# A fused block-sparse attention and gated-MLP kernel: other load sizes, one copy on another engine, and another deal of products over ten slots

## The chip, the cores and the metric

The kernel runs on one core of a Trainium2 chip. The core has a matrix engine (TensorE, PE in the profile, with its weight loads as PEld), a vector engine (VectorE, DVE), a scalar engine (ScalarE, ACT), a general engine (GpSimd, POOL), and SyncE (SP), which here only issues transfers. Each engine works through its own queue in order. Transfers run on 16 DMA engines that the queues share. The metric is the time of one execution in microseconds of device time; lower is better. The median before is 209.31 us, from three runs between 209.13 and 209.51.

## The reference

Attention with a block mask runs over 4 batches, 8 heads, 768 tokens and 64 features a head; its output, with the heads side by side (512 features), goes through a gated MLP whose gate mixes over the tokens.

```python
scores = scale * np.matmul(q, k.transpose(0, 1, 3, 2))
mask = ...                       # neighbours, first and last block, 3 sampled blocks per row of blocks
attn = softmax(np.where(mask, scores, -1000000000.0))
x = matmul(attn, v) -> [4, 768, 512]

h = np.maximum(x @ w_in, 0.0)    # 512 -> 1024
u, v = h[..., :512], h[..., 512:]
v_n = (v - mean(v)) / sqrt(var(v) + 1e-06)
v_s = np.einsum('ts,bsd->btd', w_spatial, v_n) + b_spatial[None, :, None]
out = (u * v_s) @ w_out          # 512 -> 512
```

## The kernel before, in words

Work is laid out by hand in slots. `qk_unit` (slots 0 to 35) and `qk_full` (slots 36 to 179) put one piece of scores on TensorE in each slot, into one of two PSUM buffers of the tag `sc`, and one exponential of it on ScalarE (L479, L491). `av_full` multiplies the exponentials of seven slots before with v (L538). So in a slot from 43 on, TensorE has two score matmuls (L487), six with v, and after these as many gMLP matmuls as `run_queue` takes from a queue. For slots 20 to 97 the table `STEPS` (L817) says how many; after that they are dealt evenly. At slots 82 to 91 the queue holds the output products of batch 0.

The gMLP of a batch is a list of products. For each of six rows of 128 tokens there is v0 to v5 and u0 to u5 (four matmuls with `w_in_t` each), then six matmuls with the spatial weights `w_spt` (`s_product`), then four with `w_out_t` (`o_product`). A product ends with a copy out of PSUM: relu for u and v, bias and gate for s, and for o a copy to `osb` that is then stored. `O_ACT` (L625) names, for each of the first three batches, the rows whose copy out ScalarE makes; the others go to VectorE. `ST_ACT` names the rows whose store is issued from ScalarE's queue in place of SyncE's (row 4 of batch 2). Each row of v gets mean and variance on VectorE, then 1/sqrt(var) on GpSimd (`std`, `rstd`, L657 and L659), then the normalisation on VectorE (`vn<-vn,mv,rstd`, L188).

`last_x` runs after the attention slots. It drains what is left of batch 2 and opens batch 3: three of four matmuls of v0 and v1, then the output products of rows 4 and 5 of batch 2, then three of u0, and then the fourth of each. From there gMLP products take their PSUM buffers in turn from three pools (`tail_tags`), `sc` among them; rows 3, 4 and 5 of batch 2 have `sc` buffers too, and so has u0.

The weights come in through staging tiles. The spatial weights are 768 x 768 numbers, in six pieces of 384 KB: `ws_load` (L576) fetches one or two pieces, `ws_cast` casts one to bf16 on GpSimd in slots 19 to 29, and `ws_tr` transposes a pair by DMA. `w_out` has four pieces of 256 KB: `w_out_load` in slot 44, casts on GpSimd in slot 52. SyncE issues all of these in the order of the program, between the loads of q, k and v (L110), the transposes and the stores.

Of the kernel before, what the change touches and what calls it, by code (L numbers as in the profile page):

```python
# [10 lines left out]
FP32 = mybir.dt.float32  # L11
# [15 lines left out]
def kernel(  # L27
# [16 lines left out]
    nc = tc.nc  # L44

    B, H, S, D = q.shape
# [5 lines left out]
    DM = H * D  # L52
# [3 lines left out]
    NDH = DH // 128  # L56
# [14 lines left out]
    work = ctx.enter_context(tc.tile_pool(name="work", bufs=1))  # L71
# [155 lines left out]
    wst = {}  # L227

    def w_load(key, src):
        wst[key] = work.tile([128, DM], FP32, tag="osb", bufs=6, name="w_f")  # L230
        nc.sync.dma_start(out=wst[key], in_=src)
# [13 lines left out]

    def w_out_load(g):
        w_load(("o", g), moe_w_out[g * 128:(g + 1) * 128, :])

    def w_out_cast(g, eng):
        eng.tensor_copy(out=w_out_t[:, g, :], in_=wst.pop(("o", g)))  # L250
# [323 lines left out]
    ws = {}  # L574

    def ws_load(i, n=1):  # L576
        t = work.tile([128, n, S], FP32, tag=f"ws_f{n}", bufs=2, name="ws_f")
        nc.sync.dma_start(out=t, in_=moe_w_spatial.rearrange("(p c) s -> p c s", c=NCH)[:, i:i + n])
        for k in range(n):
            ws["f", i + k] = t[:, k]  # L580
# [41 lines left out]
        return out  # L622

    NORM_AT = {1: 23, 0: 23, 3: 36, 2: 36}
    O_ACT = [(4,), (0, 2, 4), (0, 2, 4)]  # L625
    ST_ACT = [(), (), (4,), (0, 1, 2)]
    VN_AGE, VN_STEP = 9, 2
    post = []
# [1 line left out]
    class Moe:  # L630
# [75 lines left out]
        def o_product(self, tcc):  # L706
# [4 lines left out]
            for i in range(parts):  # L711
                cs = slice(i * w, (i + 1) * w)

                def done(ps, i=i, cs=cs):
                    if i == 0:
                        osb["t"] = work.tile([128, DM], FP32, tag="osb", bufs=6, name="osb")
                    on_act = (tcc + i) % 2 == 0 if self.last else tcc in O_ACT[self.b]
                    (act_copy if on_act else dve_copy)(osb["t"][:, cs], ps)
# [26 lines left out]
    def deal(steps, slots):  # L745
        queue.extend(steps)
        pace["slots"], pace["credit"] = slots, 0.0

    def run_queue(n=None):
        if n is not None:  # L750
            for _ in range(n):
                queue.popleft()()
            return
        if not queue or pace["slots"] <= 0:
            return
        pace["credit"] += (len(queue) - pace["credit"]) / pace["slots"]
        pace["slots"] -= 1
        n = int(pace["credit"] + 0.5)
        for _ in range(min(n, len(queue))):
            queue.popleft()()  # L760
            pace["credit"] -= 1
# [5 lines left out]
    def when(slot, *fns):  # L767
        at.setdefault(slot, []).extend(fns)

    def c(f, *a, **kw):  # L770
        return lambda: f(*a, **kw)
# [42 lines left out]
    when(18, lambda: first["steps"].popleft()())  # L814
    when(20, close_first)
    when(29, lambda: deal(moe[0].in_steps("v2 v3 u2 u3", TC), 14))
    STEPS = {20: 0, 21: 3, 22: 2, 23: 0, 24: 2, 25: 1, 26: 2, 27: 2, 28: 0, 29: 1, 30: 1, 31: 1, 32: 2, 33: 1, 34: 1, 35: 1, 36: 1, 37: 0, 38: 1, 39: 2, 40: 2, 41: 2, 42: 1, 43: 3, 44: 3, 45: 0, 46: 2, 47: 1, 48: 2, 49: 1, 50: 2, 51: 0, 52: 2, 53: 1, 54: 1, 55: 1, 56: 1, 57: 2, 58: 1, 59: 1, 60: 1, 61: 2, 62: 2, 63: 1, 64: 1, 65: 1, 66: 1, 67: 2, 68: 2, 69: 1, 70: 1, 71: 1, 72: 1, 73: 1, 74: 2, 75: 1, 76: 1, 77: 2, 78: 1, 79: 1, 80: 1, 81: 1, 82: 0, 83: 2, 84: 1, 85: 2, 86: 0, 87: 1, 88: 1, 89: 2, 90: 2, 91: 0, 92: 2, 93: 2, 94: 2, 95: 2, 96: 2, 97: 2}  # L817
    when(42, lambda: deal(moe[0].in_steps("v4 v5 u4 u5", TC) + moe[0].rest_steps(),
                          S0 + 8 + 48 - 42))
    for b in (1, 2):  # L820
# [24 lines left out]
    def slot_of(p):  # L845
        return S0 + 12 * (p - NG)

    for p in range(NG, NP):
        g = slot_of(p)
# [7 lines left out]
        if p == NP - 1:  # L857
            when(g + 20, last_x)
    for i, (ld, ca) in enumerate([(16, 19), (16, 21), (17, 23), (17, 25), (18, 27), (18, 29)]):
        if i not in (3, 5):  # L860
            when(ld, c(ws_load, i, 2 if i > 1 else 1))
        when(ca, c(ws_cast, i))
    for i, sl in enumerate((23, 27, 31)):
        when(sl, c(ws_tr, i))
    when(44, *[c(w_out_load, g) for g in range(NDH)])
    when(52, *[c(w_out_cast, g, PL) for g in range(NDH)])

    LAG = 7
# [6 lines left out]
    for s in range(NS + LAG + 2):  # L875
# [11 lines left out]
        for f in early:  # L887
            f()
        run_queue(STEPS.get(s))
        for f in late.get(s, []):  # L890
# [34 lines left out]
```

## Time and profile before

| | |
|---|---|
| median of three runs | 209.31 us (209.13 to 209.51) |
| profiled execution | 209.73 us, its span 208.0 us |
| ScalarE busy | 167.1 us, 80% |
| VectorE busy | 130.5 us, 63% |
| GpSimd busy | 75.4 us, 36% |
| granted clock of TensorE | 1.00 throughout |

Share of the busiest engines in three stretches of 10 us (columns: stretch, its length, then busy time and number of instructions of PE, PEld, DVE, ACT and POOL, the clock, the busy share of the DMA engines and the rate in GB/s):

```profile
30.00:40.00 10.00, 9.33 (x135) 7.41 (x134) 8.10 (x17) 9.46 (x11) 9.43 (x9) 1.00 1.22 287
80.00:90.00 10.00, 10.00 (x115) 6.17 (x113) 5.33 (x11) 9.38 (x14) 2.67 (x4) 1.00 1.12 276
180.00:190.00 10.00, 10.00 (x48) 4.46 (x47) 6.31 (x16) 6.25 (x11) 1.88 (x4) 1.00 0.52 134
```

A busy TensorE isn't TensorE at its peak: matmuls are pipelined, and one that waits in the pipe counts as busy. In rows of a timeline the columns are start and length in us, engine, line, operation, tile written and tiles read, shapes, count, and in brackets the engine's idle time before the row with what ended it.

### The profile page before, as it was taken

The page shows a single profiled execution, that of the slowest core. Times are in us where ns is not written, and L with a number is a line of the kernel's source. Part 1 is how long each engine was busy: PE and PEld are TensorE (multiplying, and loading weights), DVE is VectorE, ACT ScalarE, POOL GpSimd, SP SyncE. Part 2 cuts the span into 40 slices and gives each one's busy share as a digit, 9 for nine tenths or more (in the row PEclk, how much of TensorE's full clock was granted, in tenths as well). Part 3 has the DMA queues.
Part 4 walks back from the last instruction along what each step waited for, and adds up shares of the span by engine and source line. Part 5 has one row for each costly group of instructions (what it writes and reads, how often), then busy time and mean ns, then how long its engine had stood idle before and what let it go on. Part 6 is the DMA issues. An engine that isn't in the chain of part 4 may idle for free.

```text
span 208.0 us, 5244 instructions
## 1 busy us (share of the span) xinstructions
PE 201.7 (97%) x2122; PEld 126.3 (61%) x2122; DVE 130.5 (63%) x285; ACT 167.1 (80%) x222; POOL 75.4 (36%) x117
## 2 busy tenths in 40 slices
PE   7899999899999999999999999999999999999993
PEld 6689877665666666665556556655565556444431
DVE  7778696989654354748798355348685444386542
ACT  5999999899999999989999887998989883266021
POOL 7999599675681413310706401300202000012000
PEclk9999999999999999999999999999999999999999
DMA  5999999999999999999996649885101052960267
GB/s 149 353 367 319 307 415 262 248 260 312 282 350 188 265 266 204 369 268 248 267 129 175 169 88 273 191 237 127 38 3 38 0 91 50 161 233 0 50 145 260
DMA packets 66235, 42.41 MB, mean 204 GB/s; under 512 B 47524, under 2 KB 61220, under 8 KB 66212
## 3 DMA queue, kind: packets, MB, share of 16 engines
q1 hardware_dynamic: 65204, 40.71, 77.1%
q10 hardware_dynamic: 1008, 1.38, 1.9%
q8 instruction: 16, 0.26, 0.5%
q14 instruction: 7, 0.06, 0.1%
HBM read 24.38 MB, written 6.29 MB: 148 GB/s over the span
## 4 chain that ended last, share of the span: by engine, by line
PE 79%; DMA 12%; POOL 4%; DVE 2%; SPq 1%; ACT 0%; issue 0%; ACTq 0%; POOLq 0%
PE ps_moe L617 30%; PE ps L487 23%; PE ps_av L538 13%; DMA st_q<-in_q_dram 7%; PE ps_t L617 7%; PE ps_sc L617 4%; DMA ws_f<-in_moe_w_spatial_dram 4%; POOL ws_b L585 2%; DMA gt<-un 2%; PE wps L182 1%; DVE vn L188 1%; PE ps_av L520 1%; SPq L110 1%; DVE kq L221 1%; POOL nat L138 0%
## 5 line engine op out<-in xcount | busy, mean ns | idle before, releaser
L491 ACT ACTIVATE a_all<-ps 128x768 bf16<-128x768 f32 x144 | 112.8, 812 | 11.8 <-PE ps L487 5.4
L487 PE MATMUL ps<-kq 88*128 88x384 bf16 x288 | 70.4, 325 | 0.0
L538 PEld LDWEIGHTS <-a_all 128*128 128x128 bf16 x864 | 45.2, 97 | 20.0
L538 PE MATMUL ps_av<-vv,a_all 128*128 128x65 bf16 x864 | 49.8, 193 | 0.0
L487 PEld LDWEIGHTS <-kq 88*128 88x128 bf16 x288 | 27.7, 97 | 29.2 <-issue 0.3
L617 PE MATMUL ps_moe<-w_in_t,xt 128*128 128x512 bf16 x144 | 43.2, 378 | 0.0
L479 ACT ACTIVATE a_all<-ps 128x1024 bf16<-128x1024 f32 x36 | 34.2, 1028 | 2.7 <-PE ps L474 2.3
L617 PE MATMUL ps_moe<-vn,w_spt 128*128 128x512 bf16 x108 | 33.5, 378 | 0.0
L657 POOL TENSOR_SCALAR std<-mv 128x3 f32<-128x3 f32 (+1 forms) x9 | 2.9, 319 | 71.4 <-DVE mv L654 56.8
L138 POOL CAST nat<-st_k 128x768 bf16<-128x768 f32 (+2 forms) x18 | 14.2, 790 | 30.2 <-DMA st_k<-in_k_dram 29.3
L690 DVE SCALAR_TENSOR_TENSOR un<-ps_moe,b_col,un 128x512 bf16<-128x512 f32 x18 | 13.5, 749 | 14.8 <-PE ps_moe L617 14.8
L502 DVE RECIPROCAL rc<-ps_av 128x6 f32<-128x6 f32 (+1 forms) x36 | 6.7, 186 | 25.6 <-PE ps_av L538 23.3
L474 PE MATMUL ps<-kq 88*128 88x256 bf16 (+3 forms) x140 | 21.6, 275 | 1.0 <-ACT a_all L479 0.5
L617 PEld LDWEIGHTS <-xt 128*128 128x128 bf16 x192 | 15.4, 98 | 7.8 <-DMA xt<-xn 0.3
L503 DVE TENSOR_TENSOR xn<-ps_av,rc 128x384 bf16<-128x384 f32 (+1 forms) x36 | 18.5, 513 | 1.2
L617 PE MATMUL ps_moe<-w_out_t,gt 128*128 128x512 bf16 x60 | 17.6, 378 | 0.0
L653 DVE BATCH_NORM_STATS2 stats<-vn 128x6 f32<-128x512 bf16 x24 | 16.4, 684 | 1.2 <-ACT vn L648 0.8
L138 POOL CAST nat<-st_q 128x768 bf16<-128x768 f32 (+2 forms) x21 | 14.8, 706 | 3.3 <-DMA st_q<-in_q_dram 2.7
L474 PEld LDWEIGHTS <-kq 88*128 88x128 bf16 (+1 forms) x140 | 12.7, 97 | 5.4 <-DVE kq L221 1.0
L221 DVE COPY kq<-tt 64x1536 bf16<-64x1536 bf16 x24 | 15.1, 631 | 0.4
L188 DVE TENSOR_SCALAR vn<-ps_moe 128x512 bf16<-128x512 f32 x18 | 12.3, 686 | 4.7 <-PE ps_moe L617 4.5
L617 PEld LDWEIGHTS <-w_spt 128*128 128x128 bf16 x144 | 11.7, 98 | 5.2
(85 smaller groups left out, 207.1 us busy)
## 6 DMA issues: line engine op xcount, KB each, us to landing
st_v<-in_v_dram SPq DMA_DIRECT2D x16, 384.0 KB, 5.4
st_k<-in_k_dram SPq DMA_DIRECT2D x15, 384.0 KB, 4.3
out_dram<-osb SPq DMA_DIRECT2D x19, 256.0 KB, 2.7
st_q<-in_q_dram SPq DMA_DIRECT2D x12, 384.0 KB, 5.0
w_f<-in_moe_w_in_dram SPq DMA_DIRECT2D x6, 256.0 KB, 7.7
ws_f<-in_moe_w_spatial_dram SPq DMA_DIRECT2D x2, 768.0 KB, 10.2
w_f<-in_moe_w_out_dram SPq DMA_DIRECT2D x4, 256.0 KB, 4.0
out_dram<-osb ACTq DMA_DIRECT2D x4, 256.0 KB, 3.0
```

The lines of the kernel that those rows point to most:

```text
L138: eng.tensor_copy(out=dst, in_=src)
L188: nc.vector.tensor_scalar(out=out, in0=in0, scalar1=s1, scalar2=s2, op0=o0, **kw)
L221: nc.vector.tensor_copy(out=o, in_=i)
L474: nc.tensor.matmul(out=ps[:, at:at + n * TW], lhsT=kq[0:kr, h, ci * 128:(ci + 1) * 128], rhs=kq[0:kr, h, qcols(t0, n)], start=True, stop=True)
L479: nc.scalar.activation(out=out, in_=ps, func=AF.Exp, scale=0.125)
L487: nc.tensor.matmul(out=ps[:, hf * 512:hf * 512 + HALF], lhsT=kq[0:KR, j % H, ci * 128:(ci + 1) * 128], rhs=kq[0:KR, j % H, S + hf * HALF:S ...
L491: nc.scalar.activation(out=a_ref["h", j][:, ci, :].rearrange("p (b c) -> p b c", b=2), in_=ps.rearrange("p (b c) -> p b c", b=2)[:, :, 0:H ...
L503: nc.vector.tensor_tensor(out=out, in0=ps[:, :, 0:D], in1=rc[:, 0:n].to_broadcast([128, n, D]), op=ALU.mult)
L538: nc.tensor.matmul(out=av_ref[j][:, qc, 0:VA], lhsT=a_ref["h", j][:, ci, qc * 128:(qc + 1) * 128], rhs=vv[p % NVV][:, h, ci, 0:VA], start= ...
L617: nc.tensor.matmul(out=ref["ps"][:, 0:w], lhsT=lhs(i), rhs=rhs(i), start=(i == 0), stop=(i == n - 1))
L653: nc.vector.bn_stats(out=stats, in_=self.vn[:, tcc, :])
L690: nc.vector.scalar_tensor_tensor(out=self.un[:, tcc, :], in0=ps, scalar=b_col[:, tcc:tcc + 1], in1=self.un[:, tcc, :], op0=ALU.add, op1=AL ...
```

## The change

- `ws_load` fetches pieces 0, 1, 2 and 3 one at a time and 4 with 5 together; before, 2 with 3 were one load too. The tag of single pieces has four buffers in place of two, that of pairs one in place of two.
- A new `w_out_load2` fetches w_out's pieces 2 and 3 in one transfer, into a tile of the pairs' tag; before, all four came alone, into `osb` buffers.
- `O_ACT` for batch 2 loses row 4: VectorE copies it. Its store stays on ScalarE's queue.
- `STEPS` for slots 82 to 91 goes from 0 2 1 2 0 1 1 2 2 0 to 1 1 1 1 1 1 1 2 1 1; the sum stays 11.

```diff
+    def w_out_load2(g):
+        t = work.tile([128, 2, DM], FP32, tag="ws_f2", bufs=1, name="w_f2")
+        nc.sync.dma_start(out=t, in_=moe_w_out[g * 128:(g + 2) * 128, :].rearrange(
+            "(g p) d -> p g d", g=2))
+        wst["o", g], wst["o", g + 1] = t[:, 0], t[:, 1]
...
-        t = work.tile([128, n, S], FP32, tag=f"ws_f{n}", bufs=2, name="ws_f")
+        t = work.tile([128, n, S], FP32, tag=f"ws_f{n}", bufs=4 if n == 1 else 1, name="ws_f")
...
-    O_ACT = [(4,), (0, 2, 4), (0, 2, 4)]
+    O_ACT = [(4,), (0, 2, 4), (0, 2)]
...
-    STEPS = {
...
 82: 0, 83: 2, 84: 1, 85: 2, 86: 0, 87: 1, 88: 1, 89: 2, 90: 2, 91: 0,
...
+    STEPS = {
...
 82: 1, 83: 1, 84: 1, 85: 1, 86: 1, 87: 1, 88: 1, 89: 2, 90: 1, 91: 1,
...
-        if i not in (3, 5):
-            when(ld, c(ws_load, i, 2 if i > 1 else 1))
+        if i < 5:
+            when(ld, c(ws_load, i, 2 if i == 4 else 1))
...
-    when(44, *[c(w_out_load, g) for g in range(NDH)])
+    when(44, c(w_out_load, 0), c(w_out_load, 1), c(w_out_load2, 2))
```

More of the change, by code (lines that the diff above doesn't have):

```diff
@@ L816 @@
     when(29, lambda: deal(moe[0].in_steps("v2 v3 u2 u3", TC), 14))
-    STEPS = {20: 0, 21: 3, 22: 2, 23: 0, 24: 2, 25: 1, 26: 2, 27: 2, 28: 0, 29: 1, 30: 1, 31: 1, 32: 2, 33: 1, 34: 1, 35: 1, 36: 1, 37: 0, 38: 1, 39: 2, 40: 2, 41: 2, 42: 1, 43: 3, 44: 3, 45: 0, 46: 2, 47: 1, 48: 2, 49: 1, 50: 2, 51: 0, 52: 2, 53: 1, 54: 1, 55: 1, 56: 1, 57: 2, 58: 1, 59: 1, 60: 1, 61: 2, 62: 2, 63: 1, 64: 1, 65: 1, 66: 1, 67: 2, 68: 2, 69: 1, 70: 1, 71: 1, 72: 1, 73: 1, 74: 2, 75: 1, 76: 1, 77: 2, 78: 1, 79: 1, 80: 1, 81: 1, 82: 0, 83: 2, 84: 1, 85: 2, 86: 0, 87: 1, 88: 1, 89: 2, 90: 2, 91: 0, 92: 2, 93: 2, 94: 2, 95: 2, 96: 2, 97: 2}
+    STEPS = {20: 0, 21: 3, 22: 2, 23: 0, 24: 2, 25: 1, 26: 2, 27: 2, 28: 0, 29: 1, 30: 1, 31: 1, 32: 2, 33: 1, 34: 1, 35: 1, 36: 1, 37: 0, 38: 1, 39: 2, 40: 2, 41: 2, 42: 1, 43: 3, 44: 3, 45: 0, 46: 2, 47: 1, 48: 2, 49: 1, 50: 2, 51: 0, 52: 2, 53: 1, 54: 1, 55: 1, 56: 1, 57: 2, 58: 1, 59: 1, 60: 1, 61: 2, 62: 2, 63: 1, 64: 1, 65: 1, 66: 1, 67: 2, 68: 2, 69: 1, 70: 1, 71: 1, 72: 1, 73: 1, 74: 2, 75: 1, 76: 1, 77: 2, 78: 1, 79: 1, 80: 1, 81: 1, 82: 1, 83: 1, 84: 1, 85: 1, 86: 1, 87: 1, 88: 1, 89: 2, 90: 1, 91: 1, 92: 2, 93: 2, 94: 2, 95: 2, 96: 2, 97: 2}
     when(42, lambda: deal(moe[0].in_steps("v4 v5 u4 u5", TC) + moe[0].rest_steps(),
```

## The prediction

> **What bounds the kernel now.** I read four views in this order: the page's busy shares, TensorE's timeline around the slots that the change edits, the VectorE and GpSimd timelines where the spatial weights are cast, and the timeline of the last batch's first products.
>
> ```profile
> span 208.0 us, 5244 instructions
> PE 201.7 (97%) x2122; PEld 126.3 (61%) x2122; DVE 130.5 (63%) x285; ACT 167.1 (80%) x222; POOL 75.4 (36%) x117
> ```
>
> TensorE is busy 97% of the span. Its busy time hides small waits, because queued matmuls overlap, so the pitch of starts must be read. In the attention slots each slot opens with two score matmuls (L487), so the time from one such row to the next is the length of a slot on TensorE. The next fence is TensorE's timeline in slots 82 to 92 (the first slot with L487 is 36; columns are start, length, engine, line, operation, tiles, shapes, count). The products per slot read off the rows, none in 82, two in 83, one in 84, two in 85, none in 86, one in 87, are those of the `STEPS` table.
>
> ```profile
> 77.36 0.49 PE L487 MATMUL ps<-kq 88*128 88x384 bf16 x2
> ...
> 78.02 0.48 PE L487 MATMUL ps<-kq 88*128 88x384 bf16 x2
> ...
> 78.53 0.59 PE L617 MATMUL ps_moe<-w_out_t,gt 128*128 128x512 bf16 x2
> 78.96 0.49 PE L487 MATMUL ps<-kq 88*128 88x384 bf16 x2
> ...
> 79.47 0.38 PE L617 MATMUL ps_moe<-w_out_t,gt 128*128 128x512 bf16 x1
> 79.69 0.49 PE L487 MATMUL ps<-kq 88*128 88x384 bf16 x2
> ...
> 80.63 0.49 PE L487 MATMUL ps<-kq 88*128 88x384 bf16 x2
> ...
> 81.14 0.49 PE L487 MATMUL ps<-kq 88*128 88x384 bf16 x2
> ...
> 82.02 0.48 PE L487 MATMUL ps<-kq 88*128 88x384 bf16 x2
> ...
> 85.13 0.49 PE L487 MATMUL ps<-kq 88*128 88x384 bf16 x2
> ```
>
> A slot with no product takes 0.51 us (80.63 to 81.14), with one 0.73 (78.96 to 79.69), with two 0.94 (79.69 to 80.63). Two slots are longer than their products explain: slot 82 has none and takes 0.66 (77.36 to 78.02), slot 87 has one and takes 0.88 (81.14 to 82.02). The next fence has ScalarE's exponentials in three narrow windows, then TensorE's slot 74.
>
> ```profile
> 77.16 0.81 ACT L491 ACTIVATE a_all<-ps 128x768 bf16<-128x768 f32 x1
> 81.15 0.81 ACT L491 ACTIVATE a_all<-ps 128x768 bf16<-128x768 f32 x1
> 70.25 0.81 ACT L491 ACTIVATE a_all<-ps 128x768 bf16<-128x768 f32 x1
> 71.12 0.49 PE L487 MATMUL ps<-kq 88*128 88x384 bf16 x2
> ```
>
> Scores have two PSUM buffers, so slot 83 needs the exponential of slot 81. It ends at 77.16 + 0.81 = 77.97, and slot 83 opens 0.05 later. Slot 88 needs that of slot 86, which ends at 81.96, and opens 0.06 later. So in both places TensorE waits for ScalarE to free a buffer, 0.15 us each, because an empty slot let it run ahead. Everywhere else in the stretch it runs at its own pitch. The sum confirms it: 77.36 to 85.13 is 7.77 us for ten slots, and three empty (1.53), three single (2.19) and four double ones (3.76) make 7.48, so 0.29 is lost.
>
> The other place with a visible loss is before slot 36. These are GpSimd's rows, then VectorE's, then TensorE's:
>
> ```profile
> 29.70 4.60 POOL L585 CAST ws_b<-ws_f 128x768 bf16<-128x768 f32 x3
> ...
> 34.69 0.73 POOL L659 TENSOR_TENSOR rstd<-std,mhalf 128x2 f32<-128x2 f32 x1
> 35.38 1.57 POOL L585 CAST ws_b<-ws_f 128x768 bf16<-128x768 f32 x1
> 36.95 0.84 POOL L138 CAST nat<-st_k 128x768 bf16<-128x768 f32 x1
> 37.91 0.98 POOL L138 CAST nat<-st_q 128x768 bf16<-128x768 f32 x1
> ```
> ```profile
> 35.45 1.66 DVE L188 TENSOR_SCALAR vn<-vn,mv,rstd 128x512 bf16<-128x512 bf16 x1 [0.50 <-POOL rstd L659]
> 37.03 1.17 DVE L221 COPY kq<-tt 64x1536 bf16<-64x1536 bf16 x1
> 38.12 0.90 DVE L188 TENSOR_SCALAR vn<-vn,mv,rstd 128x512 bf16<-128x512 bf16 x1
> 38.95 0.27 DVE L221 COPY xt<-ps_av 128x256 bf16<-128x256 bf16 x1
> ...
> 46.08 0.41 DVE L188 TENSOR_SCALAR vn<-vn,mv,rstd 128x512 bf16<-128x512 bf16 x1
> 46.40 0.55 DVE L221 COPY kq<-tt 64x1536 bf16<-64x1536 bf16 x1
> ```
> ```profile
> 39.28 0.49 PE L520 MATMUL ps_av<-vv,a_all 128*128 128x65 bf16 x11 [0.67 <-DVE xt L221]
> ```
>
> TensorE waits 0.67 us for the copy of xt. On VectorE that copy is queued behind three instructions that take 1.66, 1.17 and 0.90 us, where the same operations take 0.41 and 0.55 a little later, when no GpSimd cast runs beside them. Each long one begins just after a GpSimd cast has begun and ends just after that cast ends (36.95, 37.79, 38.89). So VectorE is held by the casts, and TensorE by VectorE.
>
> **The change part by part.** The sum is made against the profiled execution's own 209.73 us (span 208.0 and 1.7 around it). That lies 0.42 above the median of the three runs shown, 209.31, and just outside their band, 209.13 to 209.51; I carry the difference over to the median.
>
> *Products one a slot.* Eleven products stay in the ten slots: nine singles and one double take 9 x 0.73 + 0.94 = 7.51 us instead of 7.77, a gain of 0.26; with the stalls read directly, 0.30. I take 0.28. The order of products is unchanged. Counted up from slot 82, only slots 82 (one ahead), 85 and 90 (one behind each) differ, so one product ends in another slot: output row 2 of batch 0, in 91 in place of 90. Its copy goes to VectorE about where it stood, and in SyncE's queue its output load-out changes places with a transpose of xt that is not read until batch 1 starts, after slot 97. I cost that at nothing. Does ScalarE keep up with singles? The run of them now goes from 78 to 88. The earlier run, slots 69 to 73, shows it: the exponential of slot 72 ends at 70.25 + 0.81 = 71.06, and slot 74 opens at 71.12, its natural pitch. So singles leave almost no slack, but no stall. Bounds: if ScalarE paced all ten slots at the pace that it kept in this stretch, 7.64 us for ten exponentials,
>
> ```profile
> 76.44 7.64 ACT L491 ACTIVATE a_all<-ps 128x768 bf16<-128x768 f32 x10
> ```
>
> the ten slots would take 7.64 and the gain would be 0.13; at best it is 0.30. From slot 92 on every slot has at least two products (0.94), where TensorE sets the pitch, so the gain travels to the end.
>
> *Output copy of row 4, batch 2.* These are ScalarE's, TensorE's and VectorE's rows there:
>
> ```profile
> 181.18 0.60 ACT L224 ACTIVATE osb<-ps_sc 128x512 f32<-128x512 f32 x1 [2.42 <-PE ps_sc L617]
> 181.81 0.35 ACTq L719 DMA_DIRECT2D out_dram<-osb  x1
> 181.85 0.81 PE L617 MATMUL ps_sc<-w_in_t,xt 128*128 128x512 bf16 x3
> 182.05 0.69 DVE L221 COPY osb<-ps_sc 128x512 f32<-128x512 f32 x1 [2.33 <-PE ps_sc L617]
> ```
>
> The copy ends at 181.78 on ScalarE. The score buffer that it frees is taken by the product after next on that pool, u0 of the last batch, at 181.85, which is exactly TensorE's pitch. VectorE is idle then and takes 0.69 for the same copy, so it ends at 181.87, and with the release of 0.06 seen above u0 starts near 181.93: 0.08 us lost. It lies between 0, if the release is quicker, and 0.09. The store stays on ScalarE's queue and now waits there for VectorE; behind it ScalarE's next work is the relu of v0, whose last matmul is queued behind u0's first three, so that wait costs nothing. What ScalarE is relieved of, 0.60 us, had nothing waiting for it.
>
> *The loads.* The load of spatial-weight pieces 2 and 3 (768 KB) becomes two transfers of 384 KB, so SyncE issues five for these weights in place of four; w_out's last two of 256 KB become one. Buffers are the same size in all. Below are the landings of the second 384 KB load and of the last 768 KB load.
>
> ```profile
> L578 SPq DMA_DIRECT2D ws_f<-in_moe_w_spatial_dram x1: 632/632/632, 22.9 to 22.9; - x1
> ...
> DMA to landing us min/median/max: 7.8/7.8/7.8
> ```
> ```profile
> L578 SPq DMA_DIRECT2D ws_f<-in_moe_w_spatial_dram x1: 647/647/647, 24.2 to 24.2; - x1
> ...
> DMA to landing us min/median/max: 10.2/10.2/10.2
> ```
>
> The second lands at 30.7, the last at 34.4, so 1,536 KB take 3.8 us, 0.95 per 384 KB; the transfers stand in line. GpSimd's three casts (4.60 us, on one another's heels from 29.70) reach the third piece at 32.73, when by this rate its pair has just landed (32.6). The split brings that piece to 31.6, but GpSimd can't take it sooner: gain 0 to 0.05. The fifth issue costs SyncE 0.63, hidden before its next instruction, a transpose at 28.66 that waits for GpSimd. If a 384 KB piece costs 1.0 instead of 0.95, all behind lands up to 0.09 later. GpSimd's cast at 37.91 is released by its load (GpSimd is free at 37.79), and it holds VectorE's 38.12 row, which holds TensorE: 0 to 0.09, I take 0.05.
>
> The Trainium skill, page DMA: Bandwidth & Descriptors, section Measured (HBM→SBUF, 128 partitions, SWDGE, issued from GpSimd), speaks against the split: it wants transfers of 1 MiB or more, and its section Anatomy of one DMA puts a fixed 2.0 us on each. By that, landings would slip 2 us and the sum would be near 211. The trace's queued transfers land about 1 us apart, so that fixed cost is not paid one by one here.
>
> The merged w_out load saves an issue that nothing waits for, and delays the third cast at most 0.13, the fourth behind it:
>
> ```profile
> 56.96 2.98 POOL L250 CAST w_out_t<-w_f 128x512 bf16<-128x512 f32 x4 [1.27 <-DMA w_f<-in_moe_w_out_dram]
> 60.15 0.83 POOL L138 CAST nat<-st_k 128x768 bf16<-128x768 f32 x1 [0.20 <-DMA st_k<-in_k_dram]
> ```
>
> The casts end at 59.94, and GpSimd then idles 0.20 for a load, which covers it; w_out is first read at slot 81. Without that cover it would cost 0.13 on GpSimd alone. I take 0.
>
> **Sum:** -0.28 + 0.08 + 0.05 + 0 = -0.15 us: 209.58 in the profiled execution's terms, 209.16 against the median.
>
> **The rivals.** *Faster: the hold between GpSimd and VectorE turns over.* GpSimd's cast of q starts 0.21 before VectorE's second vn. If later landings push it past 38.12, vn runs first, takes 0.41 and not 0.90, and TensorE resumes 0.49 sooner: 209.16 - 0.5 = 208.65. The cast of k has a smaller lead over the copy of kq (36.95 against 37.03). For it: these leads are small, and each held instruction has 0.5 to 1.25 us to give back. Against: my slip is 0.09 at most. The Trainium skill, page SBUF — State Buffer, section Who interferes with whom, calls this an exclusive lock: whoever issues first holds the port pair for the whole instruction. The rows agree (1.66 against 0.41).
>
> *Slower: the fifth transfer takes a turn of its own.* If it delays the line by 1.0 us (the spacing of two 384 KB landings) and not 0.09, GpSimd's casts, and behind them the weights' transposes and last rstd, come 1.0 later. VectorE takes the result of that rstd at 46.08; it ended at 45.93 (the fence below), so slack is 0.15, and the rest, 0.85, goes through VectorE's queue to TensorE: 209.31 - 0.20 + 0.85 = 209.96. It decides from a slip of 0.15 onward. Against it speaks the even spacing of landings.
>
> ```profile
> 45.20 0.73 POOL L659 TENSOR_TENSOR rstd<-std,mhalf 128x2 f32<-128x2 f32 x1
> ```
>
> *The smoothing does less than it says.* ScalarE keeps the pace (gain 0.13): -0.13 + 0.08 + 0.05 = 0, 209.3.
>
> **How the numbers follow.** Forecast 0.42, its own range 209.0 to 209.4; turned-over hold 0.30; fifth turn 0.16; smoothing without effect 0.12. A difference under 0.2% (0.42 us) is what a measurement here can't tell from none. Faster than that: the turned-over hold (0.30) and the forecast's lower edge (0.06), 0.36. Slower: the fifth turn and edges, 0.19. Within: 0.45. The range is 208.5 to 209.8: it takes in the turned-over hold, and leaves most of the fifth turn and the ends of the others out.
>
> **What would show it.** Right: slots 82 to 91 have no slot longer than 0.73 for one product and 0.94 for two, and slot 92 opens 7.5 us after slot 82; u0 of the last batch starts 0.08 after TensorE's pitch; TensorE's wait for xt near 39 is still 0.6 to 0.8. Wrong: a wait at a slot in the run of singles, a wait for xt under 0.3 (the faster rival) or rstd after 46.1 (the slower one), or a stall of TensorE anywhere that the trace of before has none.

## The result, and the profile after

| | before | changed |
|---|---|---|
| median of 22 runs each | 209.16 us (208.80 to 209.57) | 208.55 us (208.23 to 210.11) |
| profiled execution | 209.73 us, span 208.0 | 208.35 us, span 206.6 |

The ratio is 0.9975 (95% interval 0.9964 to 0.9985): the changed kernel is 0.52 us faster, between 0.31 and 0.75, or 0.61 by the medians. The two profiled executions differ by more, 1.4 us; where that comes from is worked out below. First the page of the changed kernel:

```profile
span 206.6 us, 5243 instructions
## 1 busy us (share of the span) xinstructions
PE 201.4 (97%) x2122; PEld 126.6 (61%) x2122; DVE 130.8 (63%) x286; ACT 166.3 (80%) x221; POOL 74.8 (36%) x117
```

TensorE's share is the same; busy time doesn't tell the two apart. VectorE has one instruction more and ScalarE one less, the moved copy. All lines behind the new function have numbers 6 higher than before (L487 is L493, L617 is L623, L690 is L696).

TensorE's score matmuls, which open slots 82, 83, 84 and so on to 92:

```profile
76.64 0.49 PE L493 MATMUL ps<-kq 88*128 88x384 bf16 x2
77.37 0.49 PE L493 MATMUL ps<-kq 88*128 88x384 bf16 x2
78.10 0.49 PE L493 MATMUL ps<-kq 88*128 88x384 bf16 x2
...
81.73 0.49 PE L493 MATMUL ps<-kq 88*128 88x384 bf16 x2
82.67 0.49 PE L493 MATMUL ps<-kq 88*128 88x384 bf16 x2
83.40 0.49 PE L493 MATMUL ps<-kq 88*128 88x384 bf16 x2
84.13 0.49 PE L493 MATMUL ps<-kq 88*128 88x384 bf16 x2
```

Slot 82 takes 0.73 us and slot 89, the one with two products, 0.94; ten slots take 84.13 - 76.64 = 7.49 instead of 7.77. Both waits for ScalarE are gone.

The products of batch 2's rows 4 and 5 (eight matmuls from 179.12) and u0 behind them on TensorE, then the moved copy on VectorE:

```profile
179.12 1.89 PE L623 MATMUL ps_sc<-w_out_t,gt 128*128 128x512 bf16 x8
180.93 0.81 PE L623 MATMUL ps_sc<-w_in_t,xt 128*128 128x512 bf16 x3
```
```profile
180.18 0.69 DVE L221 COPY osb<-ps_sc 128x512 f32<-128x512 f32 x1 [1.47 <-PE ps_sc L623]
```

Eight matmuls at 0.2155 take 1.72, so u0 would start at 180.84. It starts at 180.93, after the copy's end at 180.87: 0.09 us lost, where the prediction had sized 0.08.

GpSimd and then VectorE where the spatial weights are cast:

```profile
34.49 1.56 POOL L591 CAST ws_b<-ws_f 128x768 bf16<-128x768 f32 x1
36.87 0.83 POOL L138 CAST nat<-st_k 128x768 bf16<-128x768 f32 x1 [0.82 <-DMA st_k<-in_k_dram]
```
```profile
34.98 1.23 DVE L188 TENSOR_SCALAR vn<-vn,mv,rstd 128x512 bf16<-128x512 bf16 x1
36.13 0.54 DVE L221 COPY kq<-tt 64x1536 bf16<-64x1536 bf16 x1
36.60 0.40 DVE L188 TENSOR_SCALAR vn<-vn,mv,rstd 128x512 bf16<-128x512 bf16 x1
36.92 0.27 DVE L221 COPY xt<-ps_av 128x256 bf16<-128x256 bf16 x1
```

In this execution the cast ends at 36.05, 0.9 earlier than in the one shown of before, and GpSimd then waits 0.82 for a load. In that gap VectorE does its copy of kq and its second vn at full speed (0.54 and 0.40 in place of 1.17 and 0.90). The copy of xt comes 2.0 us earlier, and TensorE doesn't wait for it. Slot 36 opens at 40.27 instead of 40.98.

There is one more difference, in a place that the prediction didn't look at. Below are VectorE's gates of the last batch before the change (L690, one a row, here rows 2 to 4), and TensorE's two waits behind them:

```profile
195.07 0.75 DVE L690 SCALAR_TENSOR_TENSOR un<-ps_sc,b_col,un 128x512 bf16<-128x512 f32 x1 [0.54 <-PE ps_sc L617]
196.73 0.75 DVE L690 SCALAR_TENSOR_TENSOR un<-ps_t,b_col,un 128x512 bf16<-128x512 f32 x1 [0.92 <-PE ps_t L617]
197.66 0.75 DVE L690 SCALAR_TENSOR_TENSOR un<-ps_t,b_col,un 128x512 bf16<-128x512 f32 x1 [0.17 <-PE ps_t L617]
```
```profile
200.79 1.04 PE L617 MATMUL ps_sc<-w_out_t,gt 128*128 128x512 bf16 x4 [0.22 <-DMA gt<-un]
...
203.75 0.61 PE L617 MATMUL ps_sc<-w_out_t,gt 128*128 128x256 bf16 x4 [0.20 <-DMA gt<-un]
```

A product of six matmuls takes 1.29 us, so gates should be 1.29 to 1.30 apart. Row 3 starts 1.66 after row 2, and row 4 only 0.93 after row 3: row 3's gate is late by 0.37 us, though its product had ended (the trace has the release at 196.27) and VectorE had been idle since 195.82. Row 3 closes a pair, so the transpose of the pair's gated rows by DMA starts late as well, and so do the transposes behind it: SyncE issues the last three at 197.51, 198.84 and 200.15, each taking it 1.2 us (in the changed kernel at 196.22, 197.54 and 198.86). TensorE waits twice for `gt`. By the pitch of the starts (200.79 after 200.19, where 0.22 is the rule) they cost 0.38 and 0.37 us, more than the brackets say, since a matmul that is still in the pipe counts as busy. The changed kernel's rows 3 and 4:

```profile
195.44 0.75 DVE L696 SCALAR_TENSOR_TENSOR un<-ps_t,b_col,un 128x512 bf16<-128x512 f32 x1 [0.55 <-PE ps_t L623]
196.74 0.75 DVE L696 SCALAR_TENSOR_TENSOR un<-ps_t,b_col,un 128x512 bf16<-128x512 f32 x1 [0.55 <-PE ps_t L623]
```

They start 1.30 apart, 0.09 after their products, and TensorE's two waits for `gt` are all but gone: by the same pitch 0.03 and 0.07 us are left. No edit touches these instructions.

The spans of the two executions, cut at the same events (us; u0 is the first matmul of that product in the last batch):

| | to slot 36 | slots 36 to 81 | 82 to 91 | 92 to u0 | u0 to last matmul | to the end | span |
|---|---|---|---|---|---|---|---|
| before | 40.98 | 36.37 | 7.77 | 96.71 | 22.68 | 3.42 | 207.95 |
| changed | 40.27 | 36.38 | 7.48 | 96.80 | 22.04 | 3.60 | 206.57 |

### The profile page after: what moved, and what is told of

The parts are those of the page before. It is cut to its first block, busy times and chain, and to the rows that moved or that the text cites. A ratio compares the mean times of both kernels' runs of the same rounds, so it can differ in the third digit from the quotient of the medians.

```text
span 206.6 us, 5243 instructions
## 1 busy us (share of the span) xinstructions
PE 201.4 (97%) x2122; PEld 126.6 (61%) x2122; DVE 130.8 (63%) x286; ACT 166.3 (80%) x221; POOL 74.8 (36%) x117
## 4 chain that ended last, share of the span: by engine, by line
PE 94%; ACT 4%; issue 0%; DVE 0%; ACTq 0%
PE ps_moe L623 33%; PE ps L493 23%; PE ps_av L544 13%; PE ps_t L623 8%; PE ps L480 6%; PE ps_sc L623 5%; ACT a_all L485 4%; PE ps_av L526 4%; PE wps L182 1%; PE ps_av L308 1%; PE ps L308 0%; ACT kq L224 0%; PE ps L323 0%; PE mq L315 0%; ACT osb L224 0%
## 5 line engine op out<-in xcount | busy, mean ns | idle before, releaser
L493 PE MATMUL ps<-kq 88*128 88x384 bf16 x288 | 70.4, 325 | 0.0
L493 PEld LDWEIGHTS <-kq 88*128 88x128 bf16 x288 | 27.9, 97 | 29.0
L623 PE MATMUL ps_moe<-w_in_t,xt 128*128 128x512 bf16 x144 | 43.2, 378 | 0.0
L623 PE MATMUL ps_moe<-vn,w_spt 128*128 128x512 bf16 x108 | 33.5, 378 | 0.0
L696 DVE SCALAR_TENSOR_TENSOR un<-ps_moe,b_col,un 128x512 bf16<-128x512 f32 x18 | 13.5, 749 | 14.6 <-PE ps_moe L623 14.6
L623 PEld LDWEIGHTS <-xt 128*128 128x128 bf16 x192 | 15.5, 98 | 7.8 <-issue 0.2
L623 PE MATMUL ps_moe<-w_out_t,gt 128*128 128x512 bf16 x60 | 18.1, 378 | 0.0
L623 PEld LDWEIGHTS <-w_spt 128*128 128x128 bf16 x144 | 11.7, 98 | 5.2
L221 DVE COPY kq<-tt 64x1536 bf16<-64x1536 bf16 x24 | 14.6, 607 | 0.4
```

The lines of the kernel that those rows point to most:

```text
L221: nc.vector.tensor_copy(out=o, in_=i)
L493: nc.tensor.matmul(out=ps[:, hf * 512:hf * 512 + HALF], lhsT=kq[0:KR, j % H, ci * 128:(ci + 1) * 128], rhs=kq[0:KR, j % H, S + hf * HALF:S ...
L623: nc.tensor.matmul(out=ref["ps"][:, 0:w], lhsT=lhs(i), rhs=rhs(i), start=(i == 0), stop=(i == n - 1))
L696: nc.vector.scalar_tensor_tensor(out=self.un[:, tcc, :], in0=ps, scalar=b_col[:, tcc:tcc + 1], in1=self.un[:, tcc, :], op0=ALU.add, op1=AL ...
```

## The experiments

Two things were open: which edit brings the tail's 0.46 us (22.68 + 3.42 against 22.04 + 3.60) and by what way, and whether the 0.71 before slot 36 belongs to the change or to the executions. Every kernel but the last three was timed against the kernel before.

**One part each.** The first has only the new `STEPS`:

```diff
-82: 0, 83: 2, 84: 1, 85: 2, 86: 0, 87: 1, 88: 1, 89: 2, 90: 2, 91: 0,
+82: 1, 83: 1, 84: 1, 85: 1, 86: 1, 87: 1, 88: 1, 89: 2, 90: 1, 91: 1,
```

> Only the ten entries of STEPS. The forecast's term: slots 82 to 91 take 7.48 us instead of 7.77, no slot over its pitch, and the time falls by 0.28 us (ratio 0.9987). Rival, that the deal of products brings the whole measured gain: 0.5 to 0.6 us less (0.9975).

Ratio 0.9997 (0.9979 to 1.0015). The ten slots take 7.48 us and the rest is as before, 22.63 us from u0 to the last matmul. The times can't tell -0.28 from nothing, but the profile gives the term exactly, and the deal does not bring the whole gain.

The second has only the loads (`ws_load`, `w_out_load2` and their slots, as in the change).

> Only the load sizes (both the spatial weights' and w_out's). The forecast's term: 0 to 0.09 us more. Rival, that the hold between GpSimd and VectorE near 35 to 39 us turns over: TensorE's wait for xt is gone and the time falls by 0.4 to 0.6 us (0.9975). Third view, that the early landings in the changed kernel's profile were this execution's alone: the wait for xt is there in some executions of either kernel, and the medians differ by under 0.1 us.

Ratio 0.9980 (0.9966 to 0.9993), median 208.85 us: the loads do gain. But they gain in the tail, 22.03 us in place of 22.68, and not where either view had looked: slot 36 opens at 40.63.

The third has only the copy:

```diff
-    O_ACT = [(4,), (0, 2, 4), (0, 2, 4)]
+    O_ACT = [(4,), (0, 2, 4), (0, 2)]
```

> Only the output copy of row 4 of batch 2 on VectorE. The forecast's term: u0 of the last batch starts 0.08 us after TensorE's pitch, the time grows by 0.08 us (1.0004), which the times alone can hardly show. Rival, that ScalarE's relief is worth something: 0.1 us or more less.

Ratio 0.9988 (0.9977 to 1.0000): not slower. u0 does start 0.08 late, and yet u0 to the last matmul takes 22.03. (In this execution slot 92 to u0 takes 97.11, 0.40 more than before. The rest of it is a wait of TensorE for a transpose of xt near 92.6 us, which the edit doesn't touch and no other profile here has; the profiled time, 209.49, is the highest of the twelve.) In the gates of rows 2 and 3,

```profile
195.68 0.75 DVE L690 SCALAR_TENSOR_TENSOR un<-ps_sc,b_col,un 128x512 bf16<-128x512 f32 x1 [0.91 <-PE ps_sc L617]
196.61 0.75 DVE L690 SCALAR_TENSOR_TENSOR un<-ps_t,b_col,un 128x512 bf16<-128x512 f32 x1 [0.17 <-PE ps_t L617]
```

the late one is now row 2. It closes no pair, so no transpose waits for it, and row 3 is on time again (0.09 after its product). The lateness has moved by one gate, with two more instructions on VectorE: the copy and a wait of its own.

The fourth is the changed kernel with the copy back on ScalarE.

> The changed kernel with row 4 of batch 2 copied by ScalarE again. By the forecast's term 0.08 us less than the changed kernel, so 0.9971 of the kernel before where the changed kernel has 0.9975; u0 starts at TensorE's pitch. If the copy is worth something on VectorE, 0.9980 or more.

Ratio 0.9958 (0.9944 to 0.9972), median 208.33 us: the best of all, and the slot 92 to u0 stretch is 96.72 instead of 96.80. The 0.08 of the copy is there in the profile; in the times the intervals overlap.

**The place in VectorE's queue.** Counting VectorE's instructions in each trace from 0, with the waits that stand as instructions of their own, the late one is always number 319. It starts 0.40 to 0.41 us after the wait ahead of it has ended, where its neighbours take 0.04, so it is 0.35 to 0.37 us late:

| kernel | gates of rows 0 to 5 are numbers | number 319 is | from the end of the wait ahead to its start |
|---|---|---|---|
| before, e1_steps | 313 315 317 319 321 323 | gate of row 3 | 0.41, 0.40 |
| e3_copy | 315 317 319 321 323 325 | gate of row 2 | 0.41 |
| e2_loads, e4_steps_loads | 314 316 318 320 322 324 | wait ahead of the gate of row 3 | nothing seen |
| changed | 316 318 320 322 324 326 | wait ahead of the gate of row 2 | nothing seen |

If the wait ahead of a gate is the instruction that comes late, VectorE would have waited for TensorE anyway, and nothing is lost. The loads add one wait ahead of this place (three new ones and two gone, near 79 to 90 us): two pieces of w_out no longer pass through the `osb` buffers, so the first output copies take their buffers in another turn and wait for other things. To test the count by itself, the kernel before got one instruction that nothing reads:

```diff
+    pad = const.tile([128, 1], FP32)
...
+    when(60, lambda: nc.vector.memset(pad, 0.0))
```

> The kernel before with one more instruction on VectorE, a memset of one number per partition in slot 60 that nothing reads. If VectorE's 319th instruction is what comes 0.41 us late, the gate of row 3 of the last batch is now the 320th and its wait the 319th: all gates start 0.06 us after their product, TensorE's waits near 200 and 203 us are gone, u0 to the last matmul takes 22.0 us in place of 22.7, and the time falls by 0.45 us (0.998). If the loads and the copy gained the tail in another way, a memset does nothing: 22.7 us and 1.000.

Ratio 0.9974 (0.9959 to 0.9989), median 208.70 against 209.37, u0 to the last matmul 22.03, all gates 0.09 after their products:

```profile
195.43 0.75 DVE L691 SCALAR_TENSOR_TENSOR un<-ps_t,b_col,un 128x512 bf16<-128x512 f32 x1 [0.54 <-PE ps_t L618]
196.72 0.75 DVE L691 SCALAR_TENSOR_TENSOR un<-ps_t,b_col,un 128x512 bf16<-128x512 f32 x1 [0.55 <-PE ps_t L618]
```

One idle memset does what the loads did. The reverse, on the fourth kernel:

```diff
-    nc.vector.memset(past, float((NB - 1) ** 2 - 1))
+    nc.gpsimd.memset(past, float((NB - 1) ** 2 - 1))
...
+    when(60, lambda: nc.vector.memset(pad, 0.0))
```

> The changed kernel with the copy back on ScalarE, the memset of `past` moved from VectorE to GpSimd (with it goes one wait, so two instructions less on VectorE) and the same unread memset in slot 60 (one more). The gate of row 3 is then VectorE's 319th instruction again. By its place: the late gate and TensorE's two waits are back, u0 to the last matmul 22.6 us, 0.45 us more than without this (0.9986 to 0.9990 of the kernel before). If it is the loads that help: 22.0 us and 0.996 to 0.9975.

VectorE's gate of row 3 and then TensorE's waits:

```profile
196.05 0.75 DVE L697 SCALAR_TENSOR_TENSOR un<-ps_t,b_col,un 128x512 bf16<-128x512 f32 x1 [0.91 <-PE ps_t L624]
```
```profile
200.08 1.04 PE L624 MATMUL ps_sc<-w_out_t,gt 128*128 128x512 bf16 x4 [0.20 <-DMA gt<-un]
...
203.03 0.61 PE L624 MATMUL ps_sc<-w_out_t,gt 128*128 128x256 bf16 x4 [0.19 <-DMA gt<-un]
```

The late gate and both waits are back, 22.64 us from u0 to the last matmul, with the loads as in the changed kernel. The times don't settle it: the ratio, 0.9972, lies in the range of the second expectation, and its interval (0.9951 to 0.9992) takes in both. By the medians this kernel gains 0.62 us (208.75 against 209.37) and the fourth 0.98 (208.33 against 209.31). The profile does set the two apart.

The deal and the memset together, no load and no copy changed:

> The kernel before with the new deal of products and the unread memset, no load and no copy changed. If the gain is the deal (0.29 us) plus the place of VectorE's 319th instruction (0.45 us): 0.74 us less, 0.9965, as good as the changed kernel with its copy on ScalarE. If the loads are worth something themselves: 0.9985.

Ratio 0.9962 (0.9949 to 0.9975), median 208.53: as good as the fourth kernel within the intervals (some 0.3 us to either side), so the loads are worth nothing that shows, beyond the place.

The split of the spatial weights alone, which adds no wait to VectorE:

```diff
-        if i not in (3, 5):
-            when(ld, c(ws_load, i, 2 if i > 1 else 1))
+        if i < 5:
+            when(ld, c(ws_load, i, 2 if i == 4 else 1))
```

> The kernel before with the spatial weights' pieces 2 and 3 loaded one by one, w_out as before. VectorE's instructions keep their places, so by the place the tail is that of before (22.7 us from u0 to the last matmul) and the time is the same within 0.1 us. If the split itself gains, by earlier casts before slot 36, 0.998 or less.

Ratio 0.9997 (0.9988 to 1.0006); gate of row 3 late, 22.73 us. The split costs and gains nothing that can be measured.

**The first part again.** Three more executions, one time each:

> The kernel before once more, for its first part. If the wait for xt near 39 us (0.67) and the opening of slot 36 at 40.98 us are this kernel's own, they come again; if they were that execution's, slot 36 opens anywhere from 40.0 to 41.0 us. VectorE's 319th instruction is late again (22.6 to 22.7 us from u0 to the last matmul).

> The kernel before a third time, with the same two expectations: the wait for xt near 39 us comes again if it is the kernel's own, or slot 36 opens anywhere from 40.0 to 41.0 us.

> The changed kernel once more. By the loads' own effect slot 36 opens at 40.27 us again, without a wait for xt; by chance of the execution anywhere from 40.0 to 41.0. Slots 82 to 91 take 7.48 us, u0 to the last matmul 22.0.

The times are 209.59, 209.28 and 208.37 us. The gate with number 319 is late in both of the kernel before (22.66 and 22.64 us from u0 to the last matmul), and the changed kernel takes 22.04. Slot 36 opens at 40.90 and 40.64 in the kernel before and at 40.27 in the changed one. The first of TensorE's waits in the first of the three (who waited for whom: total, times, longest):

```profile
PE wps L182 <- DVE past L162: 1.0, 1, 1.0
PE ps L474 <- ACT a_all L479: 0.4, 1, 0.4
PE ps_sc L617 <- DMA gt<-un: 0.4, 2, 0.2
```

The wait for xt is not in the list, nor in that of the second or of `e1_steps`, which has the loads of before; `e3_copy`, which has them too, waits 0.26. So the 0.67 was that execution's, not the kernel's. Nor does VectorE's free second vn make the 40.27: in the changed kernel's second profile it is held again (0.91 us), and slot 36 opens at the same time. It runs free (0.40) in two of the five profiles with both loads changed, the first of the changed kernel and `e2_loads`, and in none of the other eight. Over all profiles slot 36 opens at 40.04 to 40.98 (mean of eight 40.58) with the old loads of the pairs and of w_out or with one of them alone changed, and at 40.27 to 40.63 (mean of five 40.42) with both changed. A difference of 0.16 between such spreads settles nothing: whether the loads gain a little there stays open.

## Why the prediction was right or wrong

The direction and the range held; the likeliest time, 209.16, was too high by 0.61, because a term was missing that is larger than any in the sum. Counted as a difference, 0.15 was forecast and 0.52 measured; the kernel before also came out lower here, at 209.16 instead of 209.31. That the range held is in part luck. The forecast's own range, 209.0 to 209.4, misses the time, and the lower edge of 208.5 was there for the turned-over hold, which didn't bring the gain. A gain of over 0.2%, which came, had a chance of 0.36, and a difference that doesn't show had 0.45. The parts of the change, as the cut spans give them, are -0.29 (deal), +0.09 (copy, at its place) and -0.46 (tail), together -0.66. The measured gain is 0.52 by the ratio (0.31 to 0.75).

- **Products one a slot**, -0.28 forecast: 0.29 in every kernel with the new deal. The reading by pitch of starts was right, and so was the run of singles without a stall. The rival that ScalarE sets the pace is refuted.
- **The copy**, +0.08: 0.08 to 0.09 at u0, by the buffer named. The sum called it a loss on that alone. It also puts two more instructions ahead of the last gates, and where nothing else has moved number 319 off the gate of row 3, that gains more in the tail than the copy loses (`e3_copy`: 22.03 in place of 22.68). In the changed kernel the loads have moved it already, and by the profiles the copy only costs.
- **The loads**, taken at +0.05 and 0: this is the step that failed. What it reasons about, landings and casts, changes nothing measurable (`e8_split` for the split; `e7_steps_pad` beside the fourth kernel for both loads). What it missed is that merging w_out's loads changes which `osb` buffers the output copies take and so how many waits VectorE has. That moved number 319 off the gate of row 3.
- **The reading of before.** The prediction calls the wait for xt "the other place with a visible loss". The list of TensorE's waits also has 0.4 us for `gt`, in two pieces of 0.2 that cost 0.38 and 0.37 by the pitch, and the prediction doesn't mention them. That wait is in every profile of before; the wait for xt, on which a rival and part of the range were built, is in one of three.
- **The turned-over hold** gives 208.65, close to the time measured, for a reason that isn't the change's. The hold does turn over in the first changed profile, by casts that come earlier, not later, but not in the second, and slot 36 opens at 40.27 in both. With it went the sign that TensorE's wait for xt would still be 0.6 to 0.8: it isn't there.
- **The fifth turn** didn't come: with the split alone the time is that of before, within 0.12%. The last of these loads lands at 34.5 us before and at 34.4 in the changed profile, so neither 1 us nor the 2 us that the prediction weighed against the split was lost.

Why number 319 comes late wasn't settled. It is the same number in all seven profiles in which a gate stands at that place, of row 3 or of row 2, so it goes with the place in the instruction stream and not with the row. The profiles list small loads in queues that they call instruction (queue 14 before: 7, 0.06 MB), which would fit a refill; that link is argued, not shown. Each of the thirteen profiles has one such load of 8 KB near this place, when VectorE has started 319 to 322 of its instructions, at 193.9 us in the changed kernel and at 197.7 before. But where the gate is late, that load begins 0.7 to 1.1 us after the gate has started, so it can't be what the gate waited for, and the profile doesn't say for which engine it is. The Trainium skill, page Runtime: NRT & Kernel Launch, section Instruction fetch mechanics, says that each engine's sequencer streams its instructions in blocks and that crossing from one to the next is mostly hidden. Here, if this is such a crossing, it makes VectorE 0.35 to 0.37 us late, and costs 0.46 at the end where a transpose hangs on it.

## What to carry to other kernels

When an edit can't explain a gain, cut the two spans at the same events before looking for a mechanism; the stretch that changed may be one that no edit touches. In a chain that ends the kernel, check that each instruction starts as soon after its releaser as its neighbours do: one that is late for no shown reason may be late by its number in the queue, and a single idle instruction placed ahead of it will show that. A wait seen in one profile is not yet the kernel's own; a second execution tells.

## What was not expected of the hardware

An instruction of VectorE that starts 0.35 to 0.37 us late by its place in the queue alone (number 319 here), and one memset of 128 numbers, read by nobody, that makes the kernel faster by 0.26% (0.9974, 0.9959 to 0.9989).
